# Forward and backward pass of a two-layer decode step: nine of the zero stores of the last attention issued earlier, one at a time

## The chip, the cores and the metric

The kernel runs on one core of one Trainium2 chip, and nothing else runs beside it. The metric is the device time of one execution in microseconds. A run of the kernel before took between 450.46 and 455.1 us; the median of 13 runs is 452.42 us. A profile shows one execution, with its own time.

## The reference

One token (a row `x` of 1024 bf16 values) goes through attention A, MLP B, attention A and MLP B, with the same weights in both layers, and then the gradients of everything are taken:

```python
x = A_x
x = x + A(layernorm(x)); x = x + B(layernorm(x))      # first layer  (the kernel calls them A1, B2)
x = x + A(layernorm(x)); x = x + B(layernorm(x))      # second layer (A3, B4)
# A: q = x @ wq (32 heads of 128); scores against the last 4096 of 32768 cached keys; softmax; times values; @ wo
# B: h = x @ w1 + b1; act = h * tanh(softplus(h)); act @ w2          (w1: 1024 x 3584, w2: 3584 x 1024)
outputs: x, and the gradients of x, k_cache, v_cache, wq, wo, w1, b1, w2 for a given grad_out
```

Only the last 4096 of the 32768 cached positions are attended to. The gradients of the two caches (4 x 32768 x 128 each) are therefore zero in 28672 of the 32768 positions, and these zeros have to be written to DRAM as well: 58.7 MB of the 98.58 MB that the kernel writes.

## The kernel before

**Stages.** In order of time: attention A1 forward, MLP B2 forward (`mlp_fwd`: a w1 stage, then a w2 stage), attention A3 forward, MLP B4 forward and backward in one (`mlp_turn`, seven blocks of w1), attention A3 backward (`attn_bwd` with `first` true), the second half of B4 and the backward w2 of B2 in one pass over w2 (`W2Pass`, method `rest`), B2's backward pass over w1 (`mlp_bwd_w1`), attention A1 backward (`attn_bwd` with `first` false), and at the end the tail: the weight gradients as outer products in 78 chunks (TensorE into PSUM, VectorE and ScalarE out of it into a staging slot, one store per chunk; the 16 chunks of the two cache gradients leave in stores of 1 MB, two when four chunks are ready).

**Streaming.** w1, w2 and seven of the 16 blocks of wo are loaded through six buffers, tag `st`, by loads on SP's queue (`w1_load`, `w2_load`, `wo_load`; lines 359, 353, 348 are where they are issued). A load is issued when the block six places before it has been used for the last time. In the w2 pass a chunk `c` needs, on TensorE, 16 matmuls with the transposed activation (`fwd`), eight transposes (`tp`), and eight matmuls for the gradient (`bwd`, one chunk later); on ScalarE the copy of the transposes back into the buffer (`tc`, line 633); on VectorE one multiply-and-sum with the broadcast gradient row in PSUM (`gbc`, line 647). `bcast_row` (line 593) makes `gbc`: one copy on VectorE and eight matmuls.

**Order.** The instructions of each engine stand in the order in which the program writes them (`tc.manual_schedule()`), so the place of a call is the place in the queue. In A3 backward three hooks put work of the first w2 chunks into gaps of TensorE: `copy` after the row copy, `sel` after the selecting matmuls, `ln` inside the layernorm backward. `warm(n)` issues n matmuls of 128x512 whose result nobody reads.

**Zero stores.** `zt` is a tile of zeros, and `zero_jobs` a list of 112 stores of 0.5 MB each (524,288 bytes). Two functions take from it: `zeros(n)` issues n stores on SP's queue; `bg_zeros(n, after)` issues n on POOL's queue behind a gate, a one-column copy that reads the tile `after` and so waits until that tile is written (lines 136 and 138). The table `Z` says how many stores go where. Before: 3 near the end of B2's w2 stage, 16 in A3 forward, 19 over the seven blocks of `mlp_turn`, 6 and 26 in A3 backward, 3 ahead of B2's backward w1 pass, 3 in A1 backward, all on POOL (76 in all), and the last 36 on SP by `zeros(Z["A1d"])` in A1 backward. SP's queue carries every load and every output store too, so the output stores of the tail stand behind these 36.

Of the kernel before, what the change touches and what calls it, by code (L numbers as in the profile page):

```python
# [23 lines left out]
def kernel(  # L24
# [40 lines left out]
    NW2 = TF // 2  # L65
# [61 lines left out]
    def zeros(n):  # L127
        for _ in range(min(n, len(zero_jobs))):
            nc.sync.dma_start(zero_jobs.pop(0), zt[:])  # L129
# [3 lines left out]
    def bg_zeros(n, after):  # L133

        if n:
            nc.gpsimd.tensor_copy(gate_t[:], after[:, 0:1])
        for _ in range(min(n, len(zero_jobs))):
            nc.gpsimd.dma_start(zero_jobs.pop(0), zt[:])  # L138
# [3 lines left out]
    def evac(out_ap, in_ap, cd, ca, how=None):  # L142
        if how == "v" or (how is None and ev[0] + cd <= ev[1] + ca):
            ev[0] += cd
            nc.vector.tensor_copy(out_ap, in_ap)  # L145
        else:
            ev[1] += ca
            nc.scalar.copy(out_ap, in_ap)  # L148

    def warm(n):  # L150

        ps = psum1([P, 4, P], FP32, "wps")
        for _ in range(n):
            nc.tensor.matmul(ps, lhsT=ident_bf[:], rhs=ident_bf[:, None, :].to_broadcast([P, 4, P]),
                             start=True, stop=True, skip_group_check=True)

    def shaped(t, shape):
        n = 1
        for k in shape[1:]:
            n *= k  # L160
        ap = t[0:shape[0], 0:n]
        if len(shape) == 3:
            return ap.rearrange("p (a b) -> p a b", a=shape[1])
        if len(shape) == 4:
            return ap.rearrange("p (a b c) -> p a b c", a=shape[1], b=shape[2])
        return ap

    def psum1(shape, dtype, name):
        return shaped(pt.tile([P, 512 if dtype == FP32 else 1024], dtype, name=name, tag="pt"), shape)
# [14 lines left out]
    def xpose(blocks, dst, how=None, six=False):  # L184

        n = len(blocks)
        pools["turn"] += 1
        if six and pools["turn"] % 6 > 3:
            ps = shaped(pools["top"].tile([P, 1024], BF16, name="tps", tag="h"), [P, 8, P])
        else:  # L190
            ps = psum1([P, 8, P], BF16, "tps")
        for b, ap in enumerate(blocks):
            nc.tensor.transpose(ps[:, b, :], ap, ident_bf[:])  # L193
        evac(dst, ps[:, 0:n, :].rearrange("p b c -> p (b c)"), 0.08 * n + 0.05, 0.11 * n + 0.15, how)
# [4 lines left out]
    def alt_blocks(ap2d, npair):  # L199

        return [ap2d[:, (b // 2) * 2 * P + b % 2:(b // 2) * 2 * P + b % 2 + 2 * P - 1:2] for b in range(2 * npair)], ap2d
# [26 lines left out]
    def mm(out_ap, lhsT, rhs, start, stop, **kw):  # L228
        nc.tensor.matmul(out_ap, lhsT=lhsT, rhs=rhs, start=start, stop=stop, skip_group_check=True, **kw)  # L229
# [44 lines left out]
    def level():  # L274
        ev[:] = [0.0, 0.0]
# [67 lines left out]
    def wo_load(c):  # L343
        if c < NR:
            w = wo_kept[c]
        else:
            w = strm.tile([P, 2, D], BF16, name="wo_c", tag="st")[:]
        nc.sync.dma_start(w, wo_v[c])
        return w
# [6 lines left out]
    def w1_load(i):  # L356
        t, hf = i // 2, i % 2
        w = strm.tile([P, F // 2], BF16, name="w1_c", tag="st", padded_shape=[P, 2048])
        nc.sync.dma_start(w[:], w1_v[:, t, hf * (F // 2):(hf + 1) * (F // 2)])
        return w  # L360
# [72 lines left out]
    def attn_fwd(x_col, lname, first):  # L433
# [31 lines left out]
        if not first:  # L465
            for c in range(NR, min(NO, NR + NB)):
                held[c] = wo_load(c)
            bg_zeros(Z["A3"], n_bf)
            for w in wq_t:
# [120 lines left out]
    def bcast_row(col_bf):  # L590

        rep8 = work.tile([P, TD, P], BF16, name="rep8", tag="kp")
        nc.vector.tensor_copy(rep8[:], col_bf[:, :, None].to_broadcast([P, TD, P]))
        top("two")
        big = pools["top"].tile([P, D], FP32, name="gbc")
        for t in range(TD):
            mm(big[:, t * P:(t + 1) * P], rep8[:, t, :], ident_bf[:], t % 4 == 0, True)
        return big

    hooks = {}  # L600
# [5 lines left out]
    class W2Pass:  # L606
# [33 lines left out]
        def rest(self, done, g_bf, x_col, xname, gbc, zn, last=None):  # L640
            for c in range(NW2):
                w = self.get(c)
                if c >= done:
                    self.fwd(c)
                    self.tc(c)
                scr = work.tile([P, D], BF16, name="scr", tag="kp")
                nc.vector.tensor_tensor_reduce(out=scr[:], in0=w[:, 0, :], in1=gbc[:], scale=1.0, scalar=0.0,  # L647
                                               op0=ALU.mult, op1=ALU.add, accum_out=self.wg[:, c, 0:1])
                if c:
                    self.bwd(c - 1, g_bf)  # L650
                if c == NW2 - 2 and zn:
                    bg_zeros(zn, self.wg[:, c, :])
            self.bwd(NW2 - 1, g_bf)
            if last is not None:
                last()
            x_new = keep.tile([P, TD], FP32, name=xname)
            nc.vector.tensor_add(x_new[:], x_col[:], self.acc.cols(0, TD))
            nc.vector.tensor_copy(self.wg[:, :, 1:2], self.acc.cols(TD, TD + NW2)[:, :, None])
            return x_new, self.wg

    def mlp_fwd(x_col, lname, g_bf):

        n32, n_bf, rstd = ln_fwd(x_col, lname)
        sv = dict(n32=n32, rstd=rstd)
        hacc = wide(TF)
        h_init(hacc.t, 0, TF)
        gbc = bcast_row(g_bf)
        for i in range(2 * TD):
            t, hf = i // 2, i % 2
            w = w1_load(i)  # L670
            for b in range(NW2):
                fb = hf * NW2 + b
                o = (b // 2) * 2 * P + b % 2
                mv(hacc, fb, w[:, o:o + 2 * P - 1:2], n_bf[:, t:t + 1], False, t == TD - 1)
        a_bf = pair_col("a", lname, TF)
        dact = keep.tile([P, TF], FP32, name=f"dact_{lname}")
        m = mish_exp(hacc.cols(0, TF), TF)
        w2 = W2Pass(a_bf, "wg4")
        w2.tp(0)
        mish_w(m, hacc.cols(0, TF))  # L680
        nc.vector.tensor_mul(a_bf, m["hr"], m["w_"])

        def last():
            mish_y(m)
            nc.vector.tensor_mul(dact[:], m["y"], m["r"])

        sv["dact"] = dact
        x_new, wg = w2.rest(0, g_bf, x_col, f"x_{lname}", gbc, Z["B2"], last)
        return x_new, sv, wg
# [10 lines left out]
    def mlp_turn(x_col, lname, wg, g_col, nxt):  # L700
# [30 lines left out]
        for b in range(NBK):  # L731
            bg_zeros(Z["B4"][b], dh_bf[:, lo0(b):] if b else n_bf)
            ws[b] = [w1_block(b, hh) for hh in range(2)]
# [38 lines left out]
    def mlp_bwd_w1(g_col, lname, sv, nxt):  # L772
        nacc = wide(TD)
        ws = {}

        def T(i):
            w = w1_load(i)
            ws[i] = w
            xpose(*alt_blocks(w[:, 0:1024], 4))
            xpose(*alt_blocks(w[:, 1024:1792], 3))  # L780

        def M(i, _):
            w, t, hf = ws.pop(i), i // 2, i % 2
            for b in range(NW2):
                fb = hf * NW2 + b
                mv(nacc, t, w[:, b * P:(b + 1) * P], sv["dh_bf"][:, fb:fb + 1], i == 0 and b == 0, fb == TF - 1)

        level()
        bg_zeros(Z["W1"], sv["dh_bf"])
        pipe(list(range(2 * TD)), T, M)  # L790
        return ln_bwd(nacc.cols(0, TD), sv["n32"], sv["rstd"], g_col, lname, nxt)

    def attn_bwd(g_col, g_bf, lname, sv, first, nxt):
# [4 lines left out]
        for c in range(NR, min(NO, NR + NB)):  # L798
            held[c] = wo_load(c)
        bg_zeros(Z["A3c" if first else "A1c"], g_bf)  # L800
        late = list(range(NR, NO))
# [52 lines left out]
        if first:  # L854
            pre.extend(w2_load(c) for c in range(NB))
            bg_zeros(Z["A3d"], g_bf)
            fill(100, ["V"])
# [175 lines left out]
    jobs = []  # L1033

    def run(n):
        for _ in range(min(n, len(jobs))):
            jobs.pop(0)()
# [92 lines left out]
        for _ in range(min(n, len(prep))):  # L1130
            prep.pop(0)()

    Z = dict(B2=3, A3=16, B4=[5, 2, 1, 2, 1, 2, 6], A3c=6, A3d=26, W1=3, A1c=3, A1d=36)


    x1 = None
# [39 lines left out]
    x3, sA3 = attn_fwd(x2, "A3", False)  # L1176
    g3, g3b, sB4 = mlp_turn(x3, "B4", wg4, gcol, "A3")
    w2p = W2Pass(sB4["a_bf"], "wg2")

    def w2_ahead(cs):  # L1180
        for c in cs:
            w2p.fwd(c)
            w2p.tc(c)

    hooks.update(copy=lambda: w2p.tp(0), sel=lambda: w2_ahead([0]), ln=lambda: w2_ahead([1, 2]))
    g2, g2b = attn_bwd(g3, g3b, "A3", sA3, True, "B2")
    x4, wg2 = w2p.rest(3, g2b, x3, "x_B4", bcast_row(g2b), 0)
    dh_of(wg2, "B2", sB2)
    x4_bf = keep.tile([P, TD], BF16, name="x4_bf")
    nc.vector.tensor_copy(x4_bf[:], x4[:])  # L1190
# [26 lines left out]
    dw_tall("wo", HQ, out_5.rearrange("(c p t) d -> c p t d", p=P, t=2))  # L1217
    dkv(sA3["ds"], r3("q3"), sA1["ds"], r3("q1"), out_2)
    dw_wide(lambda: area["Rq"], 512, 2048, False, out_4)
    run(6)  # L1220
    while jobs:
        zeros(1)
        run(9)
    zeros(1000)
    assert not zero_jobs

# [29 lines left out]
```

## Time and profile before

| what | value |
|---|---|
| median of 13 runs | 452.42 us (450.46 to 455.1) |
| the profiled execution: its own time | 450.74 us |
| its span, first to last instruction | 448.6 us |
| bytes read, written | 72.89 MB, 98.58 MB |
| mean over the span | 384 GB/s |
| busy: TensorE, VectorE, ScalarE, POOL | 72%, 53%, 50%, 13% |
| zero stores on POOL, on SP | 76, 36 |
| from issue to landing of a zero store (median), POOL, SP | 10.2 us, 7.7 us |

How to read it: the span is cut into 40 slices of 11.2 us in the page's second part; a row GB/s says what the 16 DMA engines moved in each, a row PEclk what clock TensorE was granted. A view by windows does the same for stretches that one chooses. In the timeline the bracket after a row says how long the engine sat idle before it and whose end it waited for. Rows of SPq are DMA issues: their length is the time over which the issues lie, not the transfers'.

### The profile page before, as it was taken

How to read it: one execution, taken by the hardware profiler on the slowest of the kernel's cores; microseconds unless marked ns; L12 is line 12 of the kernel's file. 1: busy time of each engine (PE TensorE's matmuls, PEld its weight loads, DVE VectorE, ACT ScalarE, POOL GpSimd, SP SyncE). 2: the span in 40 equal slices, each digit the busy share in tenths (PEclk: the TensorE clock that was granted, in tenths of full speed). 3: DMA queues.
4: the chain of work that ended last, by engine and by line, in shares of the span. 5: the costliest groups of instructions: out<-in, count | busy, mean ns of one | idle time of the engine just before them, and what ended most of it. 6: DMA issues, size and time to landing. Idle time of an engine off the chain costs nothing.

```text
span 448.6 us, 11941 instructions
## 1 busy us (share of the span) xinstructions
PE 323.4 (72%) x5107; PEld 220.4 (49%) x5107; DVE 236.6 (53%) x489; ACT 225.0 (50%) x262; POOL 56.6 (13%) x146
## 2 busy tenths in 40 slices
PE   0566755497997989976898687878868669897400
PEld 0333524397475989965887577855631111121000
DVE  3124101097331757674266753572359889999600
ACT  1132100075160777877475353546329899989500
POOL 2000000001430311342241020052010000000000
PEclk9999555566786999999698687999885555555555
DMA  8999997999999998999999998999999999999994
GB/s 319 385 412 423 408 409 275 403 350 339 413 415 394 392 371 299 391 411 413 417 414 410 333 350 330 312 373 417 415 416 419 419 416 417 418 419 420 418 416 186
DMA packets 52257, 172.25 MB, mean 384 GB/s; under 512 B 5200, under 2 KB 12396, under 8 KB 51180
## 3 DMA queue, kind: packets, MB, share of 16 engines
q1 hardware_dynamic: 41120, 131.61, 75.3%
q0 software_dynamic: 11040, 39.86, 22.2%
q8 instruction: 40, 0.66, 0.6%
q14 instruction: 13, 0.11, 0.1%
q10 hardware_dynamic: 44, 0.01, 0.0%
HBM read 72.89 MB, written 98.58 MB: 382 GB/s over the span
## 4 chain that ended last, share of the span: by engine, by line
PE 20%; ACT 13%; DMA 8%; issue 4%; SPq 3%; DVE 2%; DVEq 0%; POOL 0%; ACTq 0%; POOLq 0%
PE ops L229 7%; PE tps L193 6%; ACT wq_b L148 6%; DMA w_c<-in_B_w_dram 5%; PE acc L229 4%; SPq L129 3%; DMA wo_c<-in_A_wo_dram 2%; ACT st_o L148 2%; ACT K L148 2%; ACT wo_b L148 1%; DMA out_dram<-zt 1%; PE tps L623 1%; ACT V L148 1%; ACT w_c L633 1%; ACT wo_c L148 1%
## 5 line engine op out<-in xcount | busy, mean ns | idle before, releaser
L229 PEld LDWEIGHTS <-w_c 128*128 128x128 bf16 x1120 | 36.3, 102 | 20.3 <-DMA w_c<-in_B_w_dram 15.9
L138 POOL DMA_DIRECT2D out_dram<-zt x76 | 40.4, 535 | 43.0 <-DMA out_dram<-zt 40.4
L633 ACT COPY w_c<-tps 128x1024 bf16<-128x1024 bf16 x28 | 28.3, 1012 | 23.3 <-PE tps L623 14.6
L229 PE MATMUL ops<-V 2*128 2x512 bf16 (+1 forms) x160 | 34.8, 598 | 5.9 <-ACT wq_b L148 3.4
L647 DVE CUSTOM_DVE_ANT_0 scr<-w_c,gbc 128x1024 bf16<-128x1024 bf16 x28 | 34.2, 1221 | 5.6 <-DMA w_c<-in_B_w_dram 3.7
L145 DVE CAST wq_b<-ops 128x1024 bf16<-128x1024 f32 (+1 forms) x31 | 33.9, 1148 | 3.8 <-PE ops L229 3.3
L148 ACT CAST wq_b<-ops 128x1024 bf16<-128x1024 f32 (+1 forms) x33 | 33.7, 1139 | 2.2 <-PE ops L229 2.0
L148 ACT COPY K<-tps 128x1024 bf16<-128x1024 bf16 x19 | 18.6, 1019 | 27.8 <-PE tps L193 27.8
L229 PE MATMUL ops<-wo_b 2*128 2x512 bf16 x120 | 23.3, 567 | 10.9 <-ACT wq_b L148 7.2
L229 PEld LDWEIGHTS <-V 128*128 128x128 bf16 (+2 forms) x416 | 14.0, 100 | 27.8 <-issue 27.6
L623 PE MATMUL tps<-ident_bf,w_c 128*128 128x128 bf16 x224 | 23.0, 266 | 0.6 <-DMA w_c<-in_B_w_dram 0.6
L229 PE MATMUL q<-wq_b,nA_pair 128*32 128x512 bf16 x128 | 12.0, 463 | 14.8 <-DMA wq_b<-in_A_wq_dram 14.8
L148 ACT COPY w_b<-tps 128x1024 bf16<-128x1024 bf16 x20 | 19.5, 1015 | 4.9 <-PE tps L193 4.7
L145 DVE COPY K<-tps 128x1024 bf16<-128x1024 bf16 x13 | 8.8, 689 | 24.6 <-PE tps L193 24.6
L193 PE MATMUL tps<-ident_bf,w_c 128*128 128x128 bf16 x224 | 18.5, 248 | 3.7 <-DMA w_c<-in_B_w_dram 3.7
L229 PE MATMUL acc<-a_pair,w_c 128*128 128x16 bf16 x448 | 15.6, 172 | 6.2 <-DMA w_c<-in_B_w_dram 6.0
L229 PEld LDWEIGHTS <-wo_b 2*128 2x128 bf16 (+1 forms) x152 | 5.6, 99 | 29.3 <-issue 28.7
L193 PE MATMUL tps<-ident_bf,K 128*128 128x128 bf16 x256 | 19.8, 236 | 0.0
L148 ACT COPY w_c<-tps 128x768 bf16<-128x768 bf16 (+1 forms) x14 | 11.6, 829 | 16.0 <-PE tps L193 16.0
L813 DVE CUSTOM_DVE_ANT_0 wo_c<-wo_c,gbc 128x1024 bf16<-128x1024 bf16 x14 | 16.4, 1217 | 5.7 <-ACT wo_c L148 1.9
L148 ACT CAST K<-ops 128x1024 bf16<-128x1024 f32 x18 | 17.7, 1014 | 2.5 <-PE ops L229 1.8
L145 DVE COPY w_c<-tps 128x1024 bf16<-128x1024 bf16 (+1 forms) x18 | 11.7, 660 | 13.7 <-PE tps L193 9.9
(323 smaller groups left out, 664.9 us busy)
## 6 DMA issues: line engine op xcount, KB each, us to landing
out_dram<-zt POOLq DMA_DIRECT2D x76, 512.0 KB, 10.2
out_dram<-zt SPq DMA_DIRECT2D x36, 512.0 KB, 7.7
wo_c<-in_A_wo_dram SPq DMA_DIRECT2D x28, 512.0 KB, 7.9
w_c<-in_B_w_dram SPq DMA_DIRECT2D x32, 448.0 KB, 6.5
w_c<-in_B_w_dram SPq DMA_DIRECT2D x28, 512.0 KB, 6.8
out_dram<-wq_b SPq DMA_DIRECT2D x17, 512.0 KB, 11.4
wq_b<-in_A_wq_dram SPq DMA_DIRECT2D x16, 512.0 KB, 11.4
out_dram<-K SPq DMA_DIRECT2D x8, 1024.0 KB, 12.8
```

What stands on the lines that cost most here:

```text
L129: nc.sync.dma_start(zero_jobs.pop(0), zt[:])
L138: nc.gpsimd.dma_start(zero_jobs.pop(0), zt[:])
L145: nc.vector.tensor_copy(out_ap, in_ap)
L148: nc.scalar.copy(out_ap, in_ap)
L193: nc.tensor.transpose(ps[:, b, :], ap, ident_bf[:])
L229: nc.tensor.matmul(out_ap, lhsT=lhsT, rhs=rhs, start=start, stop=stop, skip_group_check=True, **kw)
L623: nc.tensor.transpose(self.ps[c][:, b, :], w[:, 1, b * P:(b + 1) * P], ident_bf[:])
L633: nc.scalar.copy(self.w[c][:, 1, :], self.ps.pop(c)[:].rearrange("p b c -> p (b c)"))
L647: nc.vector.tensor_tensor_reduce(out=scr[:], in0=w[:, 0, :], in1=gbc[:], scale=1.0, scalar=0.0, op0=ALU.mult, op1=ALU.add, accum_out=self. ...
L813: nc.vector.tensor_tensor_reduce(out=w[:, 0, :], in0=w[:, 0, :], in1=gbc[:], scale=1.0, scalar=0.0, op0=ALU.mult, op1=ALU.add, accum_out=w ...
```

## The change

The table of zero stores becomes finer. In B2's w1 stage one store is gated on the stage's input (`B2a`); in its w2 stage one store is issued after chunk 0 and one after chunk 4, besides the three after chunk 12 (`B2`). The seven numbers of `mlp_turn` change from 5, 2, 1, 2, 1, 2, 6 to 4, 2, 2, 2, 2, 2, 5. A3 backward has 27 instead of 26 in its second group. In the pass over w2 after it, one store is issued after each of chunks 1, 4, 7 and 10 (`B4w`); in B2's backward w1 pass 2 instead of 3 ahead, and one at each of steps 5 and 10, gated on the block of the step before (`W1m`). SP's block in A1 backward takes what is left: 27 instead of 36. POOL issues 85 instead of 76.

Two things besides: in B2's w1 stage `bcast_row` is called before the matmuls of the fifth block instead of ahead of the first; and in the hooks of A3 backward chunk 2 of w2 is no longer done ahead (`rest` starts with 2 chunks done instead of 3), while 3, 2 and 4 `warm` matmuls are added to the three hooks. The loop at the end of the program, which called `zeros(1)` between groups of chunks, found no stores left before; it becomes a plain run of all chunks.

```diff
-                if c == NW2 - 2 and zn:
-                    bg_zeros(zn, self.wg[:, c, :])
+                if c in zn:
+                    bg_zeros(zn[c], self.wg[:, c, :])
...
-        gbc = bcast_row(g_bf)
         for i in range(2 * TD):
             t, hf = i // 2, i % 2
             w = w1_load(i)
+            if i == 0:
+                bg_zeros(Z["B2a"], x_col)
+            if i == 4:
+                gbc = bcast_row(g_bf)
...
             w = w1_load(i)
             ws[i] = w
+            if i in Z["W1m"]:
+                bg_zeros(1, ws[i - 1])
...
-    Z = dict(B2=3, A3=16, B4=[5, 2, 1, 2, 1, 2, 6], A3c=6, A3d=26, W1=3, A1c=3, A1d=36)
+    Z = dict(B2a=1, B2={0: 1, 4: 1, NW2 - 2: 3}, A3=16, B4=[4, 2, 2, 2, 2, 2, 5], A3c=6, A3d=27, B4w={1: 1, 4: 1, 7: 1, 10: 1}, W1=2, W1m=(5, 10), A1c=3, A1d=100)
...
-    hooks.update(copy=lambda: w2p.tp(0), sel=lambda: w2_ahead([0]), ln=lambda: w2_ahead([1, 2]))
+    def copy_gap():
+        w2p.tp(0)
+        warm(3)
+
+    def sel_gap():
+        w2_ahead([0])
+        warm(2)
+
+    def ln_gap():
+        w2_ahead([1])
+        warm(4)
+
+    hooks.update(copy=copy_gap, sel=sel_gap, ln=ln_gap)
...
-    x4, wg2 = w2p.rest(3, g2b, x3, "x_B4", bcast_row(g2b), 0)
+    x4, wg2 = w2p.rest(2, g2b, x3, "x_B4", bcast_row(g2b), Z["B4w"])
...
-    run(6)
-    while jobs:
-        zeros(1)
-        run(9)
+    run(1000)
     zeros(1000)
```

## The prediction

> **What bounds the kernel now.** I read first the rows by slice of the page: where are the DMA engines full, and where not?
>
> ```profile
> PEclk9999555566786999999698687999885555555555
> DMA  8999997999999998999999998999999999999994
> GB/s 319 385 412 423 408 409 275 403 350 339 413 415 394 392 371 299 391 411 413 417 414 410 333 350 330 312 373 417 415 416 419 419 416 417 418 419 420 418 416 186
> ```
>
> From slice 27 (302 us) to slice 38 they move 415 to 420 GB/s and never pause. Below 355 GB/s are slices 6, 8, 9, 15 and 22 to 25: the w1 and w2 stages of B2, a part of `mlp_turn`, and the second w2 and w1 passes. The windows give the room there:
>
> ```profile
> 72.00:80.00 8.00, 3.90 (x128) 3.62 (x126) 0.00 (x0) 0.00 (x0) 0.00 (x0) 0.50 0.76 258
> 96.00:104.00 8.00, 6.84 (x182) 6.31 (x180) 6.68 (x13) 5.63 (x7) 0.00 (x0) 0.93 0.96 333
> ...
> 256.00:264.00 8.00, 6.29 (x169) 5.76 (x165) 6.08 (x14) 5.97 (x6) 0.00 (x0) 0.93 0.93 303
> 280.00:288.00 8.00, 7.44 (x176) 7.35 (x174) 4.56 (x8) 4.20 (x5) 0.00 (x0) 0.95 0.88 273
> ...
> 344.00:352.00 8.00, 6.24 (x30) 1.28 (x30) 7.82 (x8) 7.86 (x9) 0.00 (x0) 0.50 1.03 419
> 424.00:432.00 8.00, 0.00 (x0) 0.00 (x0) 0.00 (x0) 0.00 (x0) 0.00 (x0) 0.50 1.03 420
> ```
>
> (Columns: length; busy PE, PEld, DVE, ACT, POOL; clock; DMA share; GB/s.) In the tail DMA, DVE and ACT are all full; after 424 only DMA works, draining what has piled up. Third, the timeline of SP, DVE and ACT in the tail: what the stores wait for.
>
> ```profile
> 296.91 42.76 SPq L129 DMA_DIRECT2D out_dram<-zt  x36
> 340.39 5.78 SPq L1058 DMA_DIRECT2D out_dram<-wo_b  x5
> ...
> 335.03 5.84 DVE L145 CAST wo_b<-ops 128x1024 bf16<-128x1024 f32 x5 [0.80 <-PE ops L229]
> 369.79 4.75 DVE L145 CAST K<-ops 128x1024 bf16<-128x1024 f32 x4
> 413.85 8.01 DVE L145 CAST wq_b<-ops 128x1024 bf16<-128x1024 f32 x7 [0.18 <-PE ops L229]
> ```
>
> SP issues 36 zero stores until 339.7, then the first output. The chunks come from DVE and ACT without a long gap from 335.0 to 421.9. Last, the waits of the passes that get stores:
>
> ```profile
> 71.15 1.03 PE L229 MATMUL gbc<-ident_bf,rep 128*128 128x128 bf16 x8 [1.83 <-DVE rep L593]
> 76.06 0.55 PE L229 MATMUL acc<-nB_pair,w_c 128*128 128x16 bf16 x14 [1.65 <-DMA w_c<-in_B_w_dram]
> 102.51 0.56 PE L229 MATMUL acc<-a_pair,w_c 128*128 128x16 bf16 x16 [0.95 <-DMA w_c<-in_B_w_dram]
> 250.60 0.59 PE L229 MATMUL acc<-a_pair,w_c 128*128 128x16 bf16 x16 [4.49 <-DMA w_c<-in_B_w_dram]
> 275.07 1.67 PE L193 MATMUL tps<-ident_bf,w_c 128*128 128x128 bf16 x14 [2.69 <-DMA w_c<-in_B_w_dram]
> 287.13 0.96 PE L193 MATMUL tps<-ident_bf,w_c 128*128 128x128 bf16 x14 [0.56 <-DMA w_c<-in_B_w_dram]
> ```
>
> In the same stages in which DMA has room on average, TensorE waits for single loads. A store put there fills room or stretches such a wait.
>
> **The tail: nine stores less.** A store is 0.524 MB, 1.25 us at 418 GB/s; nine are 11.3 us. Not all of it is won. The outputs are 98.58 - 58.7 = 39.9 MB, 95.4 us at 418 GB/s. Between 440 and 448 the windows have 127 GB/s, 1.0 MB, 2.4 us at full rate: but for a trickle the outputs are through at 442.4, so their data began at 442.4 - 95.4 = 347.0. With nine fewer zeros DMA is ready for it at 335.7. But the first chunk is out of PSUM at 336.2 (the cast of 335.03 is one of five in 5.84 us); from issue to first data I take 2.0 us (the seventh w1 load, issued when PE had used the first block at about 72.4, was in at 76.06: 3.7, less 1.1 for its own bytes, bounds it at 2.6). Data then starts at 338.2: 2.5 us lost. The first 30 chunks (14 of 0.524, 16 of 0.459 MB, 14.7 MB) drain by 373.3. The next stores are the first of 1 MB, which need four chunks of the cache gradient: the row of 369.79 ends at 374.54, data at 376.5: 3.2 us lost. From there 25.2 MB, 60.3 us, so the end is 436.8 instead of 442.4: **-5.6 us**, if A1 backward ends when it does now. Each us by which it ends later is a us off this. (11.3 less 2.5 and 3.2: the nine stores are more than the tail can give back.) The emptied loop at the end issued no store before, cost nothing and hides nothing.
>
> **B2's w1 stage.** TensorE starts on w1 at 71.87, after the eight `gbc` matmuls, which wait for `rep` (0.69 us on DVE). The layernorm row is ready at 70.30. With `bcast_row` moved behind four blocks the first slot comes free 1.6 us sooner, and with it the seventh load, which TensorE waits for at 76.06; loads then follow one another at about 1.1 us. The moved 0.69 us on DVE falls into a wait of 17 us there, the 1.03 us on PE into the wait for that load: **-1.6 us**. The `B2a` store is gated at 67.9 and has data by 70; at 72 to 74 the rate is down to 59 GB/s, so it fits: 0 (up to +1.25 if it overlaps the seventh load).
>
> **B2's w2 stage.** The room at 96 to 104 is (418-333)x8 = 0.68 MB, 1.3 stores, and some earlier. But chunk 9 waits 0.95 us for its load, and later ones follow at the pace of DVE and PE, with no catching up. Per store between 0 and 1.25; I take 0.75 for each of two: **+1.5 us**.
>
> **`mlp_turn`.** 19 stores before and after. One moves from block 0 to 2, one from 6 to 4 (rates of 282 GB/s at 168 to 176). PE is busy 7.8 to 8.0 of 8 us there, except at 164 to 166 with waits of 0.76 and 0.90 us. Bounds -1 and +1.25; I take **0**.
>
> **A3 backward and the w2 pass.** The three warm matmuls of `copy` (0.21 us each at full clock) run from 236.6 to 237.3, past the row copy that ends at 236.9: 0.35 us. Two after `sel` delay the layernorm's matmul by 0.4; the four in `ln` replace the chunk taken out and end with `rep`. Chunk 2 in `rest` is 1.3 us of PE and 1.0 us of ACT, beside DVE's 1.22 us per chunk and ahead of a PE wait of 4.49 us: 0, and 1.3 if that cover were gone. The 0.75 us falls mostly into the same wait, as the loads behind it share DMA with zero stores until 248; I take 0.3. The 27th store lengthens that stretch by 1.25, the store less at the end of `mlp_turn` shortens it by up to as much: 0.5. The stores after chunks 1 and 4 are issued at 244.5 and 248.3, in a stretch at 391 to 406 GB/s, ahead of or beside the loads for which PE waits at 250.60 and again at 252.86: full price, 2.5. Those after chunks 7 and 10 meet 238 to 317 GB/s: 0.3 each. Together **+3.9 us** (0.8 to 6.3). Behind the gates POOL has only stores and the small copy of x, due at 265: nobody waits.
>
> **B2's backward w1 pass.** The three stores ahead of it run at 268 to 272 alone, before the load that PE waits for 2.69 us at 275.07; with two this is 1.25 less. The one of step 5 starts at about 273, beside loads with slack (PE takes 1.87 us a block at clock 0.5); that of step 10 meets 217 to 237 GB/s at 280 to 284 but the next loads are waited for 0.56 and 0.41 us: +0.3. **-0.95 us** (-1.25 to +1.25). Both gates read a block that has long been copied back in place, and its buffer is needed only a step later.
>
> **Two rules of the Trainium skill speak against the change.** (1) The tail runs at 415 to 420 GB/s. "DMA: Bandwidth & Descriptors", section "Where 436 GB/s comes from", says that transfers between HBM and SBUF are bound by HBM at about 358 GB/s per core. By the trace the seven windows below 340 GB/s that the stores enter (72:80, 96:112, 248:264, 272:288) have room for 758 GB/s x 8 us = 6.1 MB, 11.6 stores; by the rule 338 x 8 = 2.7 MB, 5.2 stores, and the other 3.8 would cost 1.46 us each, 5.6 in all: no gain left. The trace decides. (2) POOL's 76 store issues take 531 ns in the median and 698 at most, three of them at 108.28 between back-to-back two-input operations of DVE (line 647). "SBUF — State Buffer", "A bandwidth-pool intuition that's wrong (but worth ruling out)", has POOL's descriptor writing blocked by some VectorE copies, some 3.1 us instead of 0.62. That would make each single store land 2.5 us later and miss its gap. Again I go by the trace: 0.
>
> **Sum.** Stages: -1.6 + 1.5 + 0 + 3.9 - 0.95 = +2.85. Tail: -5.6. Together **-2.75 us**. The profiled execution took 450.74 us (span 448.6, 2.1 outside), 1.7 below the median of 452.42; the same difference on the median gives **449.7**.
>
> **Rivals.**
> - *The room is real, the stores are hidden.* For it: packets take the same time in these stages, the engines just pause between them. Then the w2 pass costs 0.8 and B2's w2 stage nothing: stages -1.6 + 0.8 - 0.95 = -1.75, tail -5.6, so -7.35: 445.1. Against it: a load in these stages lands 5 to 6 us after issue, and PE waits at its end.
> - *No change to measure* (within 0.3%, 1.4 us, which is about what a measurement of this kernel can tell): the stages lose 4.2 to 7.0 us, for instance if both stores of B2's w2 stage and all four of `B4w` cost 1.25: 452.
> - *Slower: each store costs its transfer where it is put.* Nine x 1.25 = 11.3, less 1.6 for `bcast_row`, plus 0.3 for the hooks: the stages lose 10.0, the tail returns only 5.6, +4.4: 456.8. The place is the wait at 250.60 and the chunks behind it, where five of the nine are. It decides from (5.6 + 1.6 - 0.3)/9 = 0.77 us per store. Against it: 0.77 of 1.25 is more than I find on average (0.46).
>
> That the change does not do what it says is excluded: the order of POOL's and SP's instructions has 85 and 27 stores.
>
> **How the numbers follow.** The forecast (gain of 1.4 to 5 us) 0.42, hidden 0.28, no change 0.14, slower 0.16. Faster 0.70, same 0.14, slower 0.16. The range takes in most of the hidden case and the beginning of the slower one: 445.0 to 454.6.
>
> **What would show it.** In the profile after: SP's row of zero stores x27, ending near 331; TensorE's first w1 matmul about 1.6 us sooner; the wait of 4.49 us at the seventh w2 chunk grown to 6 or 7; that of 2.69 us in the w1 pass near 1.4; the first output store issued about 337 plus the shift, and short drops in GB/s near 340 and 375, where there was none. Wrong, if the wait at 250.6 does not grow (hidden), if A1 backward ends over 5.6 us later (slower), or if the tail shows no drops (then it gives more than 5.6).

## The result, and the profile after

| | before | after |
|---|---|---|
| median | 452.86 us (48 runs, 448.93 to 459.65) | 448.93 us (11 runs, 446.57 to 451.36) |
| ratio, 95% interval | | 0.9913 [0.9889, 0.9938] |
| profiled execution: time, span | 450.74, 448.6 us | 448.5, 446.7 us |
| POOL's zero stores, SP's | 76, 36 | 85, 27 |

The changed kernel is faster by 3.9 us (2.8 to 5.0). Ratios here and below count only executions within 1.5% of the fastest of their kernel; two of the profiles used below (31 stores in SP's block, and the first of the two with 30) are of longer ones.

First the rows by slice of the changed kernel (slices counted from 0):

```profile
DMA  8999999999999999999999999999998999899997
GB/s 319 390 408 424 409 408 388 407 370 355 397 414 397 377 351 319 386 402 415 415 416 414 347 366 392 340 314 392 416 417 357 404 410 404 339 410 410 418 413 293
```

Slices 6 and 8, B2's two stages, went from 275 to 388 and from 350 to 370 GB/s: the stores are there now. In the tail, where the rate never left 415 to 420, two dips have appeared, 357 in slice 30 and 339 in slice 34, and the last slice holds 293 instead of 186. The windows of the same kernel (columns: length; busy PE, PEld, DVE, ACT, POOL; clock; DMA share; GB/s):

```profile
72.00:80.00 8.00, 3.97 (x95) 3.42 (x94) 0.00 (x0) 0.00 (x0) 0.00 (x0) 0.50 1.02 390
96.00:104.00 8.00, 6.17 (x151) 5.74 (x149) 5.66 (x10) 4.91 (x5) 0.00 (x0) 0.80 1.01 368
...
256.00:264.00 8.00, 6.91 (x152) 6.70 (x149) 5.46 (x9) 4.52 (x5) 1.22 (x4) 0.50 1.00 366
280.00:288.00 8.00, 5.95 (x119) 5.77 (x117) 2.88 (x5) 3.19 (x4) 0.96 (x3) 0.82 0.99 369
336.00:344.00 8.00, 4.17 (x35) 2.24 (x32) 4.18 (x11) 2.97 (x4) 1.67 (x6) 0.73 0.85 345
376.00:384.00 8.00, 7.60 (x56) 1.50 (x50) 7.04 (x7) 7.15 (x8) 0.00 (x0) 0.50 0.75 299
424.00:432.00 8.00, 3.15 (x14) 0.54 (x13) 4.91 (x5) 4.63 (x5) 0.00 (x0) 0.50 1.03 415
```

The DMA share in the four windows of the stages is now 0.99 to 1.02, so the engines have hardly any idle time left in these windows, and this at 366 to 390 GB/s, not at 418. The pauses of the tail are at 336 to 344 and 376 to 384. After 424 VectorE and ScalarE are still busy; less has piled up behind them than before, where only DMA worked by then. The timeline says what the pauses wait for (SP's rows, then VectorE's):

```profile
304.06 32.23 SPq L129 DMA_DIRECT2D out_dram<-zt  x27
343.39 4.94 SPq L1063 DMA_DIRECT2D out_dram<-wo_b  x5
...
342.09 5.84 DVE L145 CAST wo_b<-ops 128x1024 bf16<-128x1024 f32 x5 [0.80 <-PE ops L229]
376.85 4.75 DVE L145 CAST K<-ops 128x1024 bf16<-128x1024 f32 x4
```

SP is through with its 27 stores at 336.3, and the first chunk leaves PSUM from 342.09 on: SP now waits for the chunk, where before the chunk waited for SP. The second pause is the wait for the four chunks of 376.85. Last, TensorE's waits in the stages:

```profile
70.31 1.64 PE L229 MATMUL acc<-nB_pair,w_c 128*128 128x16 bf16 x56 [1.03 <-DVE nB_pair L295]
75.38 0.54 PE L229 MATMUL acc<-nB_pair,w_c 128*128 128x16 bf16 x14 [1.48 <-DMA w_c<-in_B_w_dram]
...
101.28 0.59 PE L229 MATMUL acc<-a_pair,w_c 128*128 128x16 bf16 x16 [0.91 <-DMA w_c<-in_B_w_dram]
...
254.48 0.60 PE L229 MATMUL acc<-a_pair,w_c 128*128 128x16 bf16 x16 [4.05 <-DMA w_c<-in_B_w_dram]
258.90 0.60 PE L229 MATMUL acc<-a_pair,w_c 128*128 128x16 bf16 x16 [0.61 <-DMA w_c<-in_B_w_dram]
265.69 0.56 PE L229 MATMUL acc<-a_pair,w_c 128*128 128x16 bf16 x16 [0.67 <-DMA w_c<-in_B_w_dram]
...
279.50 0.96 PE L193 MATMUL tps<-ident_bf,w_c 128*128 128x128 bf16 x14 [1.02 <-DMA w_c<-in_B_w_dram]
284.63 1.30 PE L193 MATMUL tps<-ident_bf,w_c 128*128 128x128 bf16 x14 [1.57 <-DMA w_c<-in_B_w_dram]
294.77 0.96 PE L193 MATMUL tps<-ident_bf,w_c 128*128 128x128 bf16 x14 [1.19 <-DMA w_c<-in_B_w_dram]
```

TensorE's first w1 matmul starts at 70.31 instead of 71.98 (the 71.87 of the prediction is its weight load). The wait of 4.49 us in the w2 pass has not grown (4.05), and small waits have come behind it. The 2.69 us of the w1 pass have become three waits of 1.0 to 1.6.

Each profile is one execution, so the times of stages below are means over the profiles of all kernels that have the same program in that stage, and the number of profiles is given.

### The profile page after: what moved, and what is told of

Read it like the earlier page. It is cut to its first block, busy times and chain, and to the rows that moved or that the text cites. A ratio compares the mean times of both kernels' runs of the same rounds, so it can differ in the third digit from the quotient of the medians.

```text
span 446.7 us, 11979 instructions
## 1 busy us (share of the span) xinstructions
PE 329.6 (74%) x5116; PEld 223.6 (50%) x5116; DVE 236.7 (53%) x489; ACT 225.1 (50%) x262; POOL 63.2 (14%) x164
## 4 chain that ended last, share of the span: by engine, by line
PE 22%; ACT 13%; DMA 9%; issue 4%; DVE 4%; POOL 1%; DVEq 0%; ACTq 0%; SPq 0%; POOLq 0%
PE ops L229 7%; DMA w_c<-in_B_w_dram 7%; PE tps L193 6%; ACT wq_b L148 6%; PE acc L229 3%; DMA wo_c<-in_A_wo_dram 2%; ACT st_o L148 2%; ACT K L148 2%; ACT wo_b L148 2%; PE d L229 1%; ACT V L148 1%; ACT wo_c L148 1%; PE sm L229 1%; PE rw L978 1%; PE tps L623 1%
## 5 line engine op out<-in xcount | busy, mean ns | idle before, releaser
L138 POOL DMA_DIRECT2D out_dram<-zt x85 | 45.2, 535 | 46.9 <-DMA out_dram<-zt 41.6
L229 PEld LDWEIGHTS <-w_c 128*128 128x128 bf16 x1120 | 37.6, 103 | 23.1 <-DMA w_c<-in_B_w_dram 17.9
L148 ACT COPY K<-tps 128x1024 bf16<-128x1024 bf16 x19 | 18.6, 1019 | 28.4 <-PE tps L193 28.4
L145 DVE COPY K<-tps 128x1024 bf16<-128x1024 bf16 x13 | 8.8, 689 | 24.6 <-PE tps L193 22.7
L229 PEld LDWEIGHTS <-wo_b 2*128 2x128 bf16 (+1 forms) x152 | 5.6, 99 | 29.3 <-issue 28.6
L148 ACT COPY w_c<-tps 128x768 bf16<-128x768 bf16 (+1 forms) x14 | 11.6, 829 | 17.1 <-PE tps L193 17.1
## 6 DMA issues: line engine op xcount, KB each, us to landing
out_dram<-zt POOLq DMA_DIRECT2D x85, 512.0 KB, 10.1
```

## The experiments

**How far two executions of one program lie apart.** Both kernels once more, unchanged.

> The kernel before once more, for its profile: how much do the stage times differ between two executions of the same program? If the differences between the two profiles (mlp_turn +1.4 us, A3 backward +1.9, the backward w1 pass +1.1 in the changed kernel) are the change's, this profile agrees with the first within 0.5 us in each. If they are scatter of single executions, it differs by 1 us or more in them. And the end: in the first profile one DMA engine alone worked from 443 to 447 us. If that belongs to this kernel, it is seen again (4 us); if it is chance, it may be gone.

> The changed kernel once more, for its profile. Theory of the floor in the tail: the end lies 101 to 102 us after the first cast of the tail, with drops in GB/s about 5 us before and some 35 us after it, and the DMA engines stop within 1 us of each other. If the stages' loss of 7 us in the first profile was scatter, A1 backward ends here nearer to 336 us (forecast: 2.85 us later than in the kernel before) and the end moves with it.

They took 456.63 and 450.63 us. In the two profiles of before, A3 backward (from the row that makes the gradient `g_B`, its input, to the row that makes `g_A`) took 49.7 and 55.0 us, `mlp_turn` 46.8 and 49.9, and SP's block began 6.4 us apart, at 296.9 and at

```profile
303.34 41.85 SPq L129 DMA_DIRECT2D out_dram<-zt  x36
```

in the second. So the 7.1 us by which the block came later in the first pair of profiles say little of the change; a stage has to be averaged over several profiles before it shows one or two us.

**The tail alone.** The nine stores are not written at all; this kernel's output lacks 4.7 MB of zeros.

```diff
-    Z = dict(..., A1c=3, A1d=36)
+    Z = dict(..., A1c=3, A1d=27)
...
-    run(6)
-    while jobs:
-        zeros(1)
-        run(9)
+    run(1000)
+    zero_jobs.clear()
     zeros(1000)
```

> The kernel before with SP's block cut from 36 to 27 stores and the nine not issued anywhere (so 4.7 MB of the zeros are not written): the tail's side of the change alone. Floor theory (outputs can't be produced sooner): -5.6 us, with pauses of DMA near 338 and 374 us. Transfers alone (DMA is the only bound of the tail): -11.3 us, no pauses. Lagging engine: if the pauses also let the slow DMA engine catch up that ends the kernel before, some 2.5 us more than the floor theory says, -8 us.

444.26 us, 0.9824 [0.9779, 0.987]: -8.0 us (-10.0 to -5.9). The full price of nine stores, 11.3, is excluded, and so, by a little, are the 5.6 that the prediction gave the tail. The windows at the pauses and at the end:

```profile
336.00:344.00 8.00, 4.60 (x29) 1.81 (x29) 5.25 (x12) 4.74 (x6) 0.52 (x1) 0.69 0.64 261
376.00:384.00 8.00, 7.63 (x54) 1.49 (x50) 7.05 (x7) 7.30 (x8) 0.00 (x0) 0.50 0.76 305
...
442.00:443.00 1.00, 0.00 (x0) 0.00 (x0) 0.00 (x0) 0.00 (x0) 0.00 (x0) 0.50 0.10 41
443.00:444.00 1.00, 0.00 (x0) 0.00 (x0) 0.00 (x0) 0.00 (x0) 0.00 (x0) 0.50 0.00 0
```

Both pauses are there, and the end is clean. The end of before is not; the same windows of one microsecond there:

```profile
442.00:443.00 1.00, 0.00 (x0) 0.00 (x0) 0.00 (x0) 0.00 (x0) 0.00 (x0) 0.50 0.36 147
443.00:444.00 1.00, 0.00 (x0) 0.00 (x0) 0.00 (x0) 0.00 (x0) 0.00 (x0) 0.50 0.07 29
444.00:445.00 1.00, 0.00 (x0) 0.00 (x0) 0.00 (x0) 0.00 (x0) 0.00 (x0) 0.50 0.06 25
446.00:447.00 1.00, 0.00 (x0) 0.00 (x0) 0.00 (x0) 0.00 (x0) 0.00 (x0) 0.50 0.06 25
```

and of the changed kernel:

```profile
443.00:444.00 1.00, 0.00 (x0) 0.00 (x0) 0.00 (x0) 0.00 (x0) 0.00 (x0) 0.50 0.49 197
444.00:445.00 1.00, 0.00 (x0) 0.00 (x0) 0.00 (x0) 0.00 (x0) 0.00 (x0) 0.50 0.06 25
445.00:446.00 1.00, 0.00 (x0) 0.00 (x0) 0.00 (x0) 0.00 (x0) 0.00 (x0) 0.50 0.00 0
```

A DMA share of 0.06 is a sixteenth, and 25 GB/s are a sixteenth of 410: for some four microseconds of before a single one of the 16 engines works. From the last moment at which 15 engines are busy to the last packet it is 5.3 to 5.8 us in the four profiles with 36 stores in SP's block, and 1.2 to 1.4 in the four with 27.

**The stages alone.** The nine stores are issued in the stages, and nine others are written a second time at the end of SP's block, so that it has 36 again.

```diff
+    again = zero_jobs[:9]
...
+            zero_jobs.extend(again)
             zeros(Z["A1d"])
```

> The changed kernel with its SP block filled up to 36 again by nine more zero stores (to places that have been written before, so 4.7 MB of zeros are written twice): the stages' side of the change alone, tail as before. Forecast: the stages lose 2.85 us net of the 1.6 that the moved bcast_row gains: +2.85 us against the kernel before. Rival, stores hidden: -1.75. Rival, each at its full transfer: +10.

460.89 us, 1.0173 [1.0123, 1.0224]: +7.8 us (5.6 to 10.1). The stages cost more than the 2.85 of the sum, and the slow engine is back. SP's row and two of the last windows:

```profile
307.35 43.25 SPq L131 DMA_DIRECT2D out_dram<-zt  x36
...
455.00:456.00 1.00, 0.00 (x0) 0.00 (x0) 0.00 (x0) 0.00 (x0) 0.00 (x0) 0.50 0.06 25
456.00:457.00 1.00, 0.00 (x0) 0.00 (x0) 0.00 (x0) 0.00 (x0) 0.00 (x0) 0.50 0.07 29
```

From the start of the block to the last packet it is 150.5 us here, as in before (149.2 to 150.2 in three profiles): what this kernel loses, it has lost by 307. A second measure of the stages is the changed kernel against the one with nine stores left out, which have the same tail: 0.9913 - 0.9824, 4.0 us with 2.4 either way. The two overlap around 6. The tail alone and the stages alone add up to -0.2, and the change gave -3.9; the difference of 3.7 has an uncertainty of 3.2 (root of the sum of the squares of 2.1, 2.2 and 1.1). So the two sides do not simply add up, if only by a little more than the uncertainty; why stays open.

**The row alone.** Before, with `bcast_row` behind four blocks.

```diff
-        gbc = bcast_row(g_bf)
         for i in range(2 * TD):
...
+            if i == 4:
+                gbc = bcast_row(g_bf)
```

> The kernel before with bcast_row in B2's w1 stage moved behind four blocks, and nothing else. Forecast's term: the w1 stage ends 1.6 us sooner, everything after it shifts, -1.6 us. Rival: the stretches in which DMA is full in A3 forward and backward swallow it, so that A1 backward ends when it did: 0.

450.46 us, 0.9943 [0.9913, 0.9973]: -2.6 us (-3.9 to -1.2). The w1 stage is the stretch from `x_A` to `y` in VectorE's timeline; in before

```profile
67.79 0.16 DVE L561 TENSOR_TENSOR x_A<-x,sm 128x8 f32<-128x8 f32 x1 [2.69 <-PE sm L229]
88.54 0.19 DVE L570 TENSOR_SCALAR y<-acc 128x28 f32<-128x28 f32 x1 [17.45 <-PE acc L229]
```

and in this kernel

```profile
67.69 0.16 DVE L561 TENSOR_TENSOR x_A<-x,sm 128x8 f32<-128x8 f32 x1 [2.69 <-PE sm L229]
87.27 0.19 DVE L570 TENSOR_SCALAR y<-acc 128x28 f32<-128x28 f32 x1 [16.27 <-PE acc L229]
```

20.75 and 19.57 us. Over all profiles it is 21.0 (three, row first) and 19.0 (ten, row later and a store beside it): 2.0 us, and the `B2a` store costs nothing. By this run the move of the row (0.69 us on VectorE, 1.0 on TensorE) brings 2.6 of the 3.9 us of the change. What is left for the nine stores, with the hooks, is 1.3, with 1.7 either way: that moving them gains anything is not shown by this difference.

**How many stores are worth moving.** Three kernels with fewer moved stores; the row is later in all, and the diffs are against the changed kernel. With two of the nine moved (one in B2's w1 stage, one more in the w1 pass, the hooks as before) 34 are left in the block, with those after chunks 7 and 10 besides, 32.

```diff
-    Z = dict(B2a=1, B2={0: 1, 4: 1, NW2 - 2: 3}, A3=16, B4=[4, 2, 2, 2, 2, 2, 5], A3c=6, A3d=27, B4w={1: 1, 4: 1, 7: 1, 10: 1}, W1=2, W1m=(5, 10), A1c=3, A1d=100)
+    Z = dict(B2a=1, B2={NW2 - 2: 3}, A3=16, B4=[5, 2, 1, 2, 1, 2, 6], A3c=6, A3d=26, B4w={}, W1=2, W1m=(5, 10), A1c=3, A1d=100)
-    hooks.update(copy=copy_gap, sel=sel_gap, ln=ln_gap)
+    hooks.update(copy=lambda: w2p.tp(0), sel=lambda: w2_ahead([0]), ln=lambda: w2_ahead([1, 2]))
...
-    x4, wg2 = w2p.rest(2, g2b, x3, "x_B4", bcast_row(g2b), Z["B4w"])
+    x4, wg2 = w2p.rest(3, g2b, x3, "x_B4", bcast_row(g2b), Z["B4w"])
```

That is two moved; four moved is the same with `B4w={7: 1, 10: 1}`.

> Of the change only: bcast_row later, the one store gated on the w1 stage's input, and in the backward w1 pass 2 stores ahead and one each at steps 5 and 10; everything else as in the kernel before. SP's block has 34. Theory now: with 30 to 36 stores the last packet comes 150 us less 1.26 per store missing after the block's first issue, so -2.5; bcast_row measured -2.6; the w1 pass has its wait of 2.69 us halved (-1.2): -6 us if the three stores are hidden there; -2.5 if each costs its 1.26 where it is.

> The same with the stores after chunks 7 and 10 of the w2 pass besides (32 in the block). The prediction priced these two at 0.3 us each: then 1.9 us faster than with two moved. If every store in the w2 pass costs its transfer, the same as with two moved.

448.35 us, 0.9917 [0.9892, 0.9942], and 447.83, 0.9923 [0.9895, 0.9952]: -3.7 and -3.5. The row and two stores bring what the row and nine bring, and two more stores add nothing that can be measured. In the profiles the pass over w2 takes 23.1 us with these two stores (mean of three) and 22.5 without any (six), and the block's time to the last packet falls from 147.1 to 145.0; that makes -1.5, and the two intervals, of 1.2 us either way, are too wide to show it. The third has 29 in the block: it is the changed kernel without the two stores of B2's w2 stage.

```diff
-    Z = dict(B2a=1, B2={0: 1, 4: 1, NW2 - 2: 3}, ...)
+    Z = dict(B2a=1, B2={NW2 - 2: 3}, ...)
```

> The changed kernel with the two single stores of B2's w2 stage back in SP's block (29). By the block's rule and the floor (the first cast is 38 us after the block's first issue, the last packet 102.7 after the cast, so 141 at the least) 29 stores give 150 - 8.8 = 141.2: as good as 27. The stages lose less by what the two cost: 1.5 us by the prediction, up to 2.5 at full transfer. So 1.5 to 2.5 us faster than the changed kernel; 2 us slower than it if the two are hidden and the tail has no floor.

446.99 us, 0.9896 [0.9861, 0.9932]: -4.7 against -3.9, not told apart. TensorE's waits for loads in that w2 stage, five in the changed kernel (0.91 the longest, above), are down to one:

```profile
99.40 0.56 PE L229 MATMUL acc<-a_pair,w_c 128*128 128x16 bf16 x16 [0.77 <-DMA w_c<-in_B_w_dram]
```

The stage takes 22.4 us in seven profiles without the two stores and 24.6 in seven with them: 2.2 us, most of their full 2.5.

**The pass over w2.** The changed kernel without its four stores there (31 in the block), and with the two later ones only and 26 instead of 27 in A3 backward (30 in the block), the latter twice.

```diff
-    Z = dict(..., A3d=27, B4w={1: 1, 4: 1, 7: 1, 10: 1}, ...)
+    Z = dict(..., A3d=27, B4w={}, ...)                   # none in the pass
+    Z = dict(..., A3d=26, B4w={7: 1, 10: 1}, ...)        # six moved
```

> The changed kernel with all four single stores of the w2 pass back in SP's block (31 there). By the prediction the four cost 3.1 us in that pass. Lagging engine and floor: the tail is 111.3 - 5 x 1.3 = 104.8, 2.1 more than with 27, so 1 us faster than the changed kernel (-5 us against before). Rival (the stores are hidden in the w2 pass): 4 x 0.95 = 3.8 us slower than the changed kernel (0 against before).

> The changed kernel with three of the nine moved stores back in SP's block (30 there): the 27th of A3 backward and those after chunks 1 and 4 of the w2 pass, which the prediction priced at full transfer. Tail from its first cast to the last packet: 36 stores gave 111.3 us (mean of three profiles), 27 gave 102.7. Theory of the lagging engine and the floor (each store less takes 1.3 us off until the floor of 102.7 is reached, after 6.6 stores): 103.5 here, and the stages lose 3.0 us less than the changed kernel's, so that it is 2 us faster than it (-6 us against the kernel before). Rival (each of the nine is worth its 0.95 us in the tail, and where they are put they cost nothing): 105.6, 3 us slower than the changed kernel (-1 us).

> The kernel with six stores moved (30 in the block) once more, since its six executions before fell apart into 442.6 (two) and 449.7 to 451.9 (four). By the block's rule the tail gives 7.5 us; if the three stores taken out of A3 backward and the w2 pass cost their transfer there, it is 2.9 us faster than the changed kernel, -6.8 us against before; if they were hidden, 1 us slower than the changed kernel, -3.

Without stores in the pass 447.75 us, 0.9873 [0.9826, 0.992]. With six moved 449.75, 0.9785 [0.9725, 0.9844] and 446.52, 0.9825 [0.977, 0.9881]. These last two ratios flatter: the twelve executions fall into two groups, five at 441.8 to 444.5 us and seven at 448.5 to 451.9, and the ratios leave out the upper one. The mean of all twelve is 446.9 us, some 1.1% below before's medians of 452.4 and 451.3 beside them and 2 us below the changed kernel's median. Its four fastest executions, 441.75 to 443.17, are the shortest of all kernels that write everything (the next is 443.25, with seven moved); that it beats the changed kernel is likely, not shown. What makes the two groups is open; of the two profiles, one from each (449.69 and 441.75 us), the longer starts SP's block 7.6 us later (304.1 and 296.5), and from there to the last packet they agree (142.3 and 142.0). The rows by slice of the shorter have one dip in the tail instead of two:

```profile
GB/s 316 382 412 425 408 409 397 406 382 382 388 415 404 388 364 347 373 403 415 416 413 416 287 397 371 387 352 401 417 416 417 417 415 408 362 409 412 417 412 303
```

With 30 stores the outputs follow the block without a pause (417 in slice 30), and only the wait for the cache gradient is left (362 in slice 34). The price in the pass itself: 22.5 us without stores, 23.1 with those after chunks 7 and 10, 25.4 with all four (five profiles). The two early ones cost 2.3 of their 2.5 us, the two late ones 0.3 each.

**The hooks.** The changed kernel with the hooks of before: no `warm` matmuls, and chunk 2 done ahead again.

```diff
-    hooks.update(copy=copy_gap, sel=sel_gap, ln=ln_gap)
+    hooks.update(copy=lambda: w2p.tp(0), sel=lambda: w2_ahead([0]), ln=lambda: w2_ahead([1, 2]))
...
-    x4, wg2 = w2p.rest(2, g2b, x3, "x_B4", bcast_row(g2b), Z["B4w"])
+    x4, wg2 = w2p.rest(3, g2b, x3, "x_B4", bcast_row(g2b), Z["B4w"])
```

> The changed kernel with the three hooks of A3 backward as before (no warm matmuls, chunks 1 and 2 both done ahead, rest starts with three done). The prediction took 0.3 us for them, as a loss of the changed kernel: -0.3 against the changed kernel. Rival: the warm matmuls keep TensorE's clock up through the w2 pass and pay: then this is 1 us or more slower than the changed kernel. In the profile the granted clock between 236 and 250 us tells.

447.85 us, 0.9904 [0.987, 0.9938]: the same as the changed kernel. The pass takes 25.3 us, as with the new hooks (25.8 and 25.3). A window ahead of it, with the old hooks:

```profile
240.00:244.00 4.00, 3.70 (x64) 2.00 (x57) 0.69 (x1) 0.00 (x0) 0.53 (x1) 1.00 1.02 416
```

A clock of 1.00 is granted there with no `warm` matmul at all. The 0.3 us that the prediction took for the hooks cannot be told from zero.

## Why the prediction was right, and where two of its terms were not

The forecast was 2.75 us less, and 3.9 (2.8 to 5.0) were measured. "Hidden" (7.35 less), "no change" and "slower" lie outside that interval. But both large terms were too small: the tail gave 2.8 us more than forecast, the stages took some 2.5 more, and the errors cancelled. That the total came near is in part luck.

**The tail: -5.6 forecast, -8.4 measured.** From the start of SP's block to the last packet it is 149.6 us in three profiles of kernels with before's tail and no stores moved, and 141.3 in three of the changed one (the two profiles and that with the old hooks). The working itself held. By the bytes left in the last slice, counted at 418 GB/s as the prediction counted 442.4, the transfers end 144.9 us after the block's start in the former and 140.0 in the latter: 4.9 less, and 5.6 were forecast. What the rate lacks of 418 GB/s in slices 28 to 38 adds up to 5.3, 5.8 and 6.1 us in the three profiles of the latter, where two pauses of 2.5 and 3.2 were forecast, at the places named. The step that failed is one half-sentence: "but for a trickle the outputs are through at 442.4". The trickle was the critical path. An execution ends with its last packet, and in before that is the packet of one engine, 5.6 us after the others. In a tail with pauses the last engine ends 1.3 us after the others, so the program gains the pauses back there: they cost the engines that wait, and hardly the one that is behind. The two profiles of one program, the one with 30 stores in the block, show it. First the longer execution, which has hardly a pause in the tail, and a window 2.4 us before its last packet (446.4):

```profile
381.00:382.00 1.00, 0.70 (x11) 0.18 (x8) 0.94 (x1) 1.00 (x2) 0.00 (x0) 0.50 0.95 385
444.00:445.00 1.00, 0.00 (x0) 0.00 (x0) 0.00 (x0) 0.00 (x0) 0.00 (x0) 0.50 0.07 29
```

then the shorter, with a pause, and a window that holds its last packet (438.5):

```profile
375.00:376.00 1.00, 0.98 (x10) 0.23 (x8) 0.28 (x2) 1.00 (x2) 0.00 (x0) 0.50 0.17 70
438.00:439.00 1.00, 0.00 (x0) 0.00 (x0) 0.00 (x0) 0.00 (x0) 0.00 (x0) 0.50 0.07 25
```

In the pause the share falls to 0.17: two or three engines still work while the rest have run out. From the last moment with 15 engines busy to the last packet it is 4.2 us without the pause and 1.6 with it, though the rate lacks 0.6 us in the one and 2.5 in the other; both tails are 142 us long. This is one pair of executions, and no run changed the pauses on purpose.

**How many stores the tail can give back.** From the block's start to the last packet: 149.2 to 150.5 us with 36 stores, 147.1 with 34, 145.0 with 32, 141.9 with 31, 142.3 and 142.0 with 30, 142.1 with 29, 140.7 to 142.1 with 27 (36 and 27 in four profiles each, the others in one or two). It falls with each store until about 31 and hardly further: from there on the tail is about as long as the chunks take. "More than the tail can give back" was right for nine; five or six would have been enough, and the last three only cost in the stages.

**The stages: +2.85 forecast, +5.3 in the profiles.** SP's block begins at 300.4 us on average in before's two profiles and that with the stores left out, and at 305.7 in the four kernels with all nine in the stages. Since single executions differ by six us, this is good to about 2.5; the kernel with 36 in the block says 7.8 (5.6 to 10.1). By term:

| stage | forecast | measured (profiles) |
|---|---|---|
| B2 w1: row later, one store | -1.6 | -2.0 (3 and 10) |
| B2 w2: two stores | +1.5 | +2.2 (7 and 7) |
| A3 forward and `mlp_turn` | 0 | +2.0, about 1.4 either way (6 and 8) |
| A3 backward | about +0.8 of the 3.9 | not visible in a scatter of 49.7 to 55.0 |
| w2 pass | about +3.1 of the 3.9 | +2.9 (6 and 5) |
| B2 backward w1 pass | -0.95 | about 0 |

Three terms were mis-sized: the two stores of B2's w2 stage, the w1 pass, and A3 forward with `mlp_turn`, which was put at nothing. The prediction read the room of a stage as 418 GB/s less the rate of a window, and 418 is what full engines move in the tail. The DMA share, which stood in the same rows, says for how long they are idle. By stages, before:

```profile
67.80:88.50 20.70, 9.64 (x235) 8.21 (x235) 1.86 (x8) 0.50 (x2) 0.00 (x0) 0.50 0.89 334
88.50:111.30 22.80, 19.93 (x449) 18.88 (x448) 19.04 (x38) 14.39 (x15) 2.19 (x5) 0.65 0.96 351
...
143.30:190.00 46.70, 43.91 (x988) 43.48 (x989) 31.35 (x124) 35.53 (x45) 11.53 (x27) 0.95 1.00 362
...
239.70:263.50 23.80, 17.40 (x410) 16.37 (x406) 18.26 (x33) 13.16 (x13) 0.00 (x0) 0.78 0.95 350
263.50:292.70 29.20, 24.03 (x456) 22.88 (x457) 13.64 (x29) 11.60 (x14) 2.45 (x6) 0.82 0.93 336
```

and after:

```profile
67.70:86.90 19.20, 9.78 (x236) 8.28 (x235) 1.91 (x9) 0.50 (x2) 0.89 (x2) 0.50 1.02 395
86.90:111.30 24.40, 20.45 (x448) 19.13 (x448) 19.03 (x39) 14.39 (x15) 3.45 (x9) 0.64 1.02 371
...
243.70:269.60 25.90, 18.51 (x413) 16.74 (x410) 18.30 (x32) 13.16 (x13) 2.87 (x8) 0.74 0.99 365
```

`mlp_turn` (143.3 to 190.0) has a share of 1.00 at 362 GB/s, and after the change B2's w2 stage and the w2 pass have 1.02 and 0.99 at 371 and 365. So near-full engines move less in these stages than 418. The packets in before's trace say how. In `mlp_turn` some 6,340 of 8,850 data packets are of 1024 bytes and take 46 ns in the median, 22 GB/s per engine; those of 4096 bytes take 159 ns, 26 GB/s, there as in the tail. By these medians full engines would move 388 GB/s in `mlp_turn`, which is about half of the way from the tail's rate to its 362. In B2's w2 stage the packets of the loads have 4096 bytes and the same median, but one in twenty takes over 1.3 times as long, which brings their mean to 177 ns (160 in the tail); why these take longer the trace does not say.

The idle time before was 2.3 us in B2's w1 stage (0.11 of 20.7), 0.9 in its w2 stage, 1.2 in the w2 pass and 2.0 in the w1 pass: 6.4 us, five stores of 1.25, where the prediction's rates gave room for 11.6. A share can exceed 1 for a while, since packets overlap, and then hides idle time elsewhere; summed over windows of 1 us it is 7.8 us, six stores. The one store in the w1 stage cost nothing; two in the w2 stage cost 2.2 of their 2.5 us, and four in the w2 pass 2.9 of their 5.0. So far it looks as if what goes beyond the idle time is paid. Other executions do not bear that out. The w2 pass in the second profile of before, and in the kernel with 36 stores in the block, which has four stores in the pass:

```profile
247.60:269.10 21.50, 16.60 (x409) 15.32 (x405) 18.23 (x31) 13.06 (x13) 0.00 (x0) 0.84 0.78 272
248.10:274.10 26.00, 19.39 (x413) 17.69 (x410) 18.24 (x32) 13.16 (x13) 2.88 (x8) 0.67 0.85 313
```

The first has 4.7 us of idle time, room for nearly four stores; the second is the longest w2 pass of all fourteen profiles, and its engines are idle for 3.9 us of it all the same. Idle time somewhere in a stage does not make a store free, and the w1 pass, with its 2.0 us idle, did not get cheaper by the store less ahead of it.

- In B2's w2 stage 0.75 us per store was taken between 0 and 1.25; it is 1.1.
- The w1 pass was to gain 0.95 us and takes 28.4 us in four profiles before and 28.6 in ten after. In the first pair of profiles the wait of 2.69 us did become shorter (1.02), but waits of 1.57 and 1.19 us came at 284.63 and 294.77, behind the two stores gated inside the pass. These were put at 0.3; no run has them without the store less ahead, so that they take the gain back is a reading of this pair.
- The landing times in "lands 5 to 6 us after issue" were read low: in before's profile the medians in these stages are 5.1 to 8.2 us. No term rests on them.
- For `mlp_turn` nothing was forecast, since the number of stores stays at 19. The 2.0 us are a difference between groups of profiles, and no run changed these seven numbers alone: whether they cause it was not tried.
- In the w2 pass the sum was right (2.5 for the early two, 0.6 for the late two), the place was not: the wait of 4.49 us was to grow to 6 or 7, and became 4.05 with others behind it. By the prediction's own mark, "wrong, if the wait at 250.6 does not grow", the stores would have been hidden, and they were not. A single wait of one execution is no mark for what a pass loses; its length, averaged over several executions, is.

**The two rules.** On the first, the Trainium skill ("DMA: Bandwidth & Descriptors", "Where 436 GB/s comes from") has HBM bind at about 358 GB/s per core. Against it, the tail still runs at 404 to 420 outside its pauses, with only this core at work, and so does B2's w1 stage, at 395 over 19 us after the change. The other stages move 359 to 371 with near-full engines, close to the rule's figure, but in `mlp_turn` the small packets above account for about half of that without it. By its size the prediction's count by the rule, room for 5.2 stores, is nearer to the idle time found (five or six) than its count by the trace (11.6); as a limit the rule is contradicted, so the nearness is no support for it. On the second, the 85 store issues of POOL take 531 ns in the median and 696 at most. The 3.1 us of "SBUF — State Buffer", "A bandwidth-pool intuition that's wrong (but worth ruling out)", do not occur here: zero was right. (Line 647 reads one of its two operands from PSUM, so this need not be the page's case.)

## What to carry to other kernels

The difference between the rate of a stage and that of another stage overstates the room for a transfer: look at the DMA share, which says how long the engines are idle, and at the size of the packets. Even idle time does not make a transfer free; what it costs is seen in the length of the stage over several executions (two stores cost 2.2 of their 2.5 us in a stage with a share of 0.96). Count first how much the place that is relieved can give back (here five or six stores) and move no more. And look at the end of a drain engine by engine: a last DMA share of 0.06 is one engine of 16 at work, and here it lasted for four microseconds.

## What was not expected of the hardware

- DMA engines at a share of 0.99 to 1.03 move 415 to 420 GB/s in before's tail and 359 to 371 in `mlp_turn`, B2's w2 stage and the w2 pass; packets of 1024 bytes take 46 ns in the median, those of 4096 bytes 159.
- After some 145 us of full queues one DMA engine of 16 is behind the others by 5.3 to 5.8 us, in all four profiles with 36 stores in the block; with 34, 32 and 31 it is 4.9, 4.6 and 2.5, with 30 once 4.2 and once 1.6, with 27 to 29 1.2 to 1.4. Which engine it is, and why, the records here do not say.
- Executions of one program on one core scatter over 10 us (448.93 to 459.65 in 48 runs of before), and a stage without any change by 5 (A3 backward, 49.7 and 55.0).
- The kernel with six stores moved has two groups of executions, five up to 444.5 us and seven from 448.5, with none between.
